# Second layer of the second mixture: seven half-size products in place of eight for 1792 of 2304 tokens

## The chip, the cores and the metric

The kernel runs on one core of a Trainium2 chip. Its time is the device time of one execution in microseconds, given as the median of several runs.

## What is computed

An attention (pooled and local) gives `x` of 2304 tokens by 512. Two feed-forward mixtures follow, both 512 to 2048 to 512. The change is in the last product of the second.

```python
def _moe2_ref(x, w_in, w_out, s, b) -> np.ndarray:
    h = x @ w_in
    r = np.maximum(h, 0.0)
    g = s * (r * r) + b
    return (g @ w_out).astype(np.float32)
```

All is float32. The kernel makes one float32 product from three matmuls in a reduced format: each operand is cut into a high part and the small rest, and high by high, high by low and low by high are summed.

## The kernel before

Five engines work beside each other: TensorE (PE; its weight loads are listed as PEld), VectorE (DVE), ScalarE (ACT), GpSimd (hardly used) and the queue of SyncE (SP), which issues nearly all transfers.

The kernel writes down its operations with `op(engine, cost, function, w, r, pr)`: what is written and read, and a priority. A planner (`Weave.plan`) then places them one by one on the engines by these costs, and this fixes the order in which each engine executes. Buffers come from named kinds with a fixed number of slots; for kinds in the list given to `Weave`, buffers take slots in the order in which they were written down. An engine executes in its order: an instruction that waits holds up all that stand behind it. An operation of `EITHER` may be placed on ACT or DVE.

Tokens go in blocks of 512 (the last of 256). The second mixture has two stages.

**Its first layer** (`group`, `late`, `w_sums`) already uses seven products in place of eight. It writes `g` to HBM (`g_dram`, listed as `gd`). `w_sums` loads a plain weight tile `f` of 128x512 into one of four staging slots (kind `st`), makes sums and cuts them into high and low parts.

**Its second layer** runs over blocks and, in each, over the 16 slices of 128 of the 2048 features. Per slice and block: `graw` comes back from HBM, ACT casts it to `gh`, DVE subtracts to `gl`, and PE makes, for each of 128 tokens, one product of three matmuls with 512 columns into one of four PSUM banks `o`. The stationary operand is a 128x128 tile of `gh` or `gl`; the 512 columns are a weight tile `wo`. All 16 `wo` tiles (high and low) are made once, in the first block, by `w_out` and `halves`, and stay in SBUF. Finished banks are copied to `os` and stored.

```python
def product(t, n, lhs, rhs, w, r, first, last, pr, **kw):

    def fn():
        for i in range(3):
            nc.tensor.matmul(t(), lhsT=lhs(i), rhs=rhs(i), start=(first and i == 0), stop=(last and i == 2), **kw)
```

That `product` is line 831 of the profile; all matmuls of both mixtures are recorded under it. Line 1112 is the cast to `gh`, line 1113 the subtraction to `gl`, line 387 the low half of a weight tile, line 996 a sum of `w_sums`, line 327 a copy or cast on either engine, line 340 a transfer.

Of the kernel before, what the change touches and what calls it, by code (L numbers as in the profile page):

```python
# [8 lines left out]
F32 = mybir.dt.float32  # L9
# [7 lines left out]
P = 128  # L17
CH = 18
# [253 lines left out]
def kernel(ctx, tc, q, k, v, w1_in, w1_out, w2_in, w2_out, s2, b2, cst, out):  # L272
# [37 lines left out]
    W = Weave(kinds, ("lq", "lk", "lv", "xf", "xh", "xl", "upT", "sc", "le", "bank", "u", "yr", "st"))  # L310
# [28 lines left out]
    def dma(out, in_, eng=None, **kw):  # L339
        (eng or nc.sync).dma_start(out=out, in_=in_, **kw)  # L340
# [44 lines left out]
    def halves(f, o, pr, more=0.0):  # L385
        op(EITHER, (0.52 + more, 0.34 + more), lambda eng: copy(eng, o[:, 0], f[:].bitcast(F32)), w=[(o, 0)], r=[f], pr=pr)
        op("dve", 0.6 + more, lambda: nc.vector.tensor_tensor(
            out=o[:, 1], in0=f[:].bitcast(F32), in1=o[:, 0].bitcast(F32), op=ALU.subtract), w=[(o, 1)], r=[f, (o, 0)], pr=pr - 0.001)
# [444 lines left out]
        op("pe", 3 * pe(n), fn, w=w, r=r, pr=pr, table="mix")  # L833
# [153 lines left out]
    def plain(nm, m, kind, after, pr):  # L987
        f = Buf(kind, [P, KD, P], F32, "f32")
        op("sp", (1, 0.8), lambda: dma(f[:], w_dram[nm][m]), w=[f], r=[(w_dram[nm], m)] + after, pr=pr)
        return f  # L990

    def w_sums(m, pr, after):
        f, g = [plain("in", m + a * HF, "st", after, pr) for a in range(2)]
        d, e = [Buf("st", [P, KD, P], F32, "sum") for _ in range(2)]
        def plus(out, a, b, by, w, r):
            op("dve", dve(2 * P) + MORE, lambda: nc.vector.tensor_tensor(out=out(), in0=a(), in1=b(), op=by), w=[w], r=r, pr=pr)

        half = lambda t, i: (lambda: t[:, 2 * i:2 * i + 2])
# [91 lines left out]
    wo2 = {}  # L1090

    def w_out(m, pr):
        f = plain("out", m, "st", [(sums[HF - 1][3], 0)], pr)
        wo2[m] = Buf("u", [P, 2, KD, P], F32R, "wo")
        halves(f, wo2[m], pr, MORE)

    for j, (c0, n) in enumerate(blocks):
        nt = n // P
        os_ = [Buf("bank", [P, DM], F32, f"o{d}") for d in range(nt)]
        for q in range(HF):  # L1100
            if j == 0:
                w_out(q, 40 + 2 * q)
                w_out(q + HF, 41 + 2 * q)
            graw = Buf("u", [P, 2, n], F32, "graw")
            op("sp", (1, 1.6 * n / NB), lambda graw=graw, q=q, j=j: dma(graw[:], g_dram[j].tile[q::HF].rearrange("f p n -> p f n")),
               w=[graw], r=[(g_dram[j], q), (g_dram[j], q + HF)], pr=41 + 20 * j + 2 * q)
            for a in range(2):
                m = q + a * HF
                wo = wo2[m]
                gh = Buf("gh", [P, n], F32R, "gh2")  # L1110
                gl = Buf("gl", [P, n], F32R, "gl2")
                op("act", act(n), lambda graw=graw, gh=gh, a=a: nc.scalar.copy(out=gh[:], in_=graw[:, a]), w=[gh], r=[graw], pr=-5 + j * 0.1)  # L1112
                op("dve", dve(n), lambda graw=graw, gh=gh, gl=gl, a=a: nc.vector.tensor_tensor(  # L1113
                    out=gl[:], in0=graw[:, a], in1=gh[:].bitcast(F32), op=ALU.subtract), w=[gl], r=[graw, gh], pr=-5 + j * 0.1)
                for d in range(nt):
                    sl = slice(d * P, (d + 1) * P)
                    product(lambda d=d, os_=os_: os_[d][:], DM, lambda i, gh=gh, gl=gl, sl=sl: (gl if i == 2 else gh)[:, sl],
                            lambda i, wo=wo: wo[:, i % 2].rearrange("p k f -> p (k f)"), [os_[d]], [wo, gh, gl], q == 0 and a == 0, q == HF - 1 and a == 1,
                            LP + 300 + j * 10)
        for d in range(nt):  # L1120
            o = Buf("ys", [P, DM], F32, "os")
            op(EITHER, (act(DM), dve(DM)), lambda eng, o=o, d=d, os_=os_: copy(eng, o[:], os_[d][:]),
               w=[o], r=[os_[d]], pr=-5)
            r0 = c0 + d * P
            whole = min(max(NBAND * S - r0, 0), P)

            def store(o=o, r0=r0, whole=whole):
                if whole:
                    dma(out[r0:r0 + whole], o[:whole])
                for i in range(whole // NCH, P // NCH):  # L1130
                    b, r = divmod(r0 + i * NCH, S)
                    dma(out[b * S:(b + 1) * S].rearrange("(c s) e -> s c e", s=CH)[r // NCH], o[i * NCH:(i + 1) * NCH])

            op("sp", (1 if whole == P else 4, 0.9), store, r=[o], pr=-5)
# [49 lines left out]
```

## Time and profile before

| | |
|---|---|
| median of 3 runs | 906.52 us (904.98 to 906.55) |
| the profiled execution | 908.74 us, its span 906.9 us |
| granted TensorE clock, mean | 0.995 |
| PE busy | 879.2 us (97%) |
| DVE busy | 664.3 us (73%) |
| ACT busy | 441.6 us (49%) |

The span runs from the first to the last instruction in the trace; the execution's own time has 1.84 us more around it. Busy times are sums over the span, so they tell nothing of single stages.

### The profile page before, as it was taken

How to read it: one execution, taken by the hardware profiler on the slowest of the kernel's cores; microseconds unless marked ns; L12 is line 12 of the kernel's file. 1: busy time of each engine (PE TensorE's matmuls, PEld its weight loads, DVE VectorE, ACT ScalarE, POOL GpSimd, SP SyncE). 2: the span in 40 equal slices, each digit the busy share in tenths (PEclk: the TensorE clock that was granted, in tenths of full speed). 3: DMA queues.
4: the chain of work that ended last, by engine and by line, in shares of the span. 5: the costliest groups of instructions: out<-in, count | busy, mean ns of one | idle time of the engine just before them, and what ended most of it. 6: DMA issues, size and time to landing. Idle time of an engine off the chain costs nothing.

```text
span 906.9 us, 13852 instructions
## 1 busy us (share of the span) xinstructions
PE 879.2 (97%) x5016; PEld 718.2 (79%) x5016; DVE 664.3 (73%) x1266; ACT 441.6 (49%) x956; POOL 0.2 (0%) x4
## 2 busy tenths in 40 slices
PE   7899999999999999999999999999999999999997
PEld 6677767777777877787878988888888888888885
DVE  6999997799999999898778988777687322222222
ACT  5965785755547323432234665555567322223232
POOL 0000000000000000000000000000000000000000
PEclk9989999999999999999999999999999999999999
DMA  9999312453333221446998433434279962201011
GB/s 192 257 296 252 108 44 56 134 150 89 113 81 83 93 73 33 139 153 217 301 311 282 136 105 128 154 140 136 105 243 329 385 227 93 70 24 30 17 36 35
DMA packets 129389, 132.66 MB, mean 146 GB/s; under 512 B 64684, under 2 KB 90922, under 8 KB 129322
## 3 DMA queue, kind: packets, MB, share of 16 engines
q1 hardware_dynamic: 129010, 131.49, 47.7%
q8 instruction: 39, 0.64, 0.3%
q10 hardware_dynamic: 312, 0.30, 0.1%
q14 instruction: 28, 0.23, 0.1%
HBM read 95.06 MB, written 36.70 MB: 145 GB/s over the span
## 4 chain that ended last, share of the span: by engine, by line
PE 58%; DVE 27%; DMA 7%; ACT 4%; issue 3%; SPq 1%; DVEq 0%; ACTq 0%
PE o L831 22%; PE ha L831 10%; PE hp L831 10%; PE y L831 7%; PE hc L831 5%; DVE tmp L513 3%; DMA w_raw<-in_moe_w_out_dram 2%; DVE gl L853 2%; PE hb L831 2%; DVE tmp L476 2%; DVE f L381 2%; DVE sc L479 2%; DVE f L378 2%; DVE tmp L518 2%; DVE f L375 1%
## 5 line engine op out<-in xcount | busy, mean ns | idle before, releaser
L831 PE MATMUL hp<-xh,wi 128*128 128x512 f32 (+1 forms) x640 | 201.6, 379 | 2.2 <-ACT g L851 1.6
L831 PE MATMUL y<-gh,wo 128*128 128x512 f32 (+1 forms) x640 | 201.1, 377 | 0.0
L831 PE MATMUL o<-wo,gh 128*128 128x512 f32 x576 | 177.3, 389 | 0.0
L1113 DVE TENSOR_TENSOR gl<-graw,gh 128x512 fp32r<-128x512 f32 (+1 forms) x80 | 51.0, 639 | 136.4 <-ACT gh L1112 130.3
L831 PEld LDWEIGHTS hp<-xh,wi 128*128 128x128 f32 x640 | 117.1, 189 | 27.2 <-ACT g L851 6.2
L831 PEld LDWEIGHTS y<-gh,wo 128*128 128x128 f32 x640 | 117.1, 189 | 19.4 <-issue 0.4
L831 PEld LDWEIGHTS o<-wo,gh 128*128 128x128 f32 x576 | 108.1, 188 | 22.4
L831 PE MATMUL y<-gl,wo 128*128 128x512 f32 (+1 forms) x320 | 118.9, 372 | 2.7 <-DVE gl L853 2.5
L831 PE MATMUL hp<-xl,wi 128*128 128x512 f32 (+1 forms) x320 | 118.6, 371 | 1.0 <-DVE xl L554 1.0
L1112 ACT CAST gh<-graw 128x512 fp32r<-128x512 f32 (+1 forms) x80 | 46.4, 581 | 135.6 <-PE o L831 135.3
L831 PE MATMUL o<-wo,gl 128*128 128x512 f32 x288 | 112.0, 389 | 0.0
L852 ACT CAST gh<-g 128x512 fp32r<-128x512 f32 (+1 forms) x80 | 46.2, 577 | 94.6 <-PE y L831 93.0
L831 PE MATMUL ha<-yh,wi 128*128 128x512 f32 x256 | 87.1, 390 | 0.0
L851 ACT ACTIVATE g<-hp 128x512 f32<-128x512 f32 (+1 forms) x80 | 44.5, 556 | 61.6 <-DVE gl L853 56.7
L831 PEld LDWEIGHTS y<-gl,wo 128*128 128x128 f32 x320 | 60.5, 189 | 13.9 <-DVE gl L853 5.8
L831 PEld LDWEIGHTS hp<-xl,wi 128*128 128x128 f32 x320 | 60.5, 189 | 9.6 <-DVE xl L554 1.6
L831 PEld LDWEIGHTS o<-wo,gl 128*128 128x128 f32 x288 | 54.1, 188 | 11.3
L1013 DVE SCALAR_TENSOR_TENSOR g<-g 128x512 f32<-128x512 f32 (+1 forms) x80 | 49.4, 635 | 10.5 <-ACT g L1012 9.6
L831 PEld LDWEIGHTS ha<-yh,wi 128*128 128x128 f32 x256 | 48.1, 188 | 9.6
L853 DVE TENSOR_TENSOR gl<-g,gh 128x512 fp32r<-128x512 f32 (+1 forms) x80 | 50.4, 630 | 4.1 <-ACT gh L852 3.9
L831 PE MATMUL ha<-yl,wi 128*128 128x512 f32 x128 | 50.0, 390 | 0.0
L327 ACT COPY g<-ha 128x512 f32<-128x512 f32 x47 | 27.6, 587 | 42.1 <-PE ha L831 37.7
(153 smaller groups left out, 1351.0 us busy)
## 6 DMA issues: line engine op xcount, KB each, us to landing
gd<-g SPq DMA_DIRECT2D x64, 256.0 KB
graw<-gd SPq DMA_DIRECT2D x32, 512.0 KB
wi_raw<-in_moe_w_in_dram SPq DMA_DIRECT2D x16, 512.0 KB
wo_raw<-in_moe_w_out_dram SPq DMA_DIRECT2D x16, 512.0 KB
w_raw<-in_moe_w_in_dram SPq DMA_DIRECT2D x16, 512.0 KB
w_raw<-in_moe_w_out_dram SPq DMA_DIRECT2D x16, 512.0 KB
nq<-in_q_dram SPq DMA_DIRECT2D x32, 144.0 KB
nk<-in_k_dram SPq DMA_DIRECT2D x32, 144.0 KB
```

Source lines behind the costliest of these rows:

```text
L327: (nc.scalar.copy if eng == "act" else nc.vector.tensor_copy)(out=out, in_=in_)
L378: op("dve", 0.6 + more, lambda: nc.vector.scalar_tensor_tensor(out=f[:], in0=t[:, :, :, 1], scalar=-0x40000000, in1=f[:], op0=ALU.bitwise_ ...
L381: op("dve", 0.6 + more, lambda: nc.vector.scalar_tensor_tensor(out=f[:], in0=t[:, :, :, 0], scalar=29, in1=f[:], op0=ALU.logical_shift_rig ...
L476: op("dve", dve(n * WIN * D), lambda t=t, i0=i0, n=n, h2=h2: nc.vector.tensor_tensor(out=t[:], in0=wide(qs[:, h2, i0:i0 + n, :].unsqueeze( ...
L513: op("dve", dve(n * WIN * D), lambda t=t, i0=i0, n=n, h2=h2: nc.vector.tensor_tensor(out=t[:], in0=wide(e[:, h2 * ns + i0:h2 * ns + i0 + n ...
L831: nc.tensor.matmul(t(), lhsT=lhs(i), rhs=rhs(i), start=(first and i == 0), stop=(last and i == 2), **kw)
L851: op("act", act(n), lambda g=g, hp=hp: nc.scalar.activation(out=g[:], in_=hp[:], func=AF.Silu), w=[g], r=[hp], pr=-5, table="silu")
L852: op("act", act(n), lambda g=g, gh=gh: nc.scalar.copy(out=gh[:], in_=g[:]), w=[gh], r=[g], pr=-5)
L853: op("dve", dve(n), lambda g=g, gh=gh, gl=gl: nc.vector.tensor_tensor(out=gl[:], in0=g[:], in1=gh[:].bitcast(F32), op=ALU.subtract), w=[gl ...
L1013: op("dve", dve(n) + 1.5 * MORE, lambda: nc.vector.scalar_tensor_tensor(out=t[:], in0=t[:], scalar=0.0, in1=t[:], op0=ALU.max, op1=ALU.mul ...
L1112: op("act", act(n), lambda graw=graw, gh=gh, a=a: nc.scalar.copy(out=gh[:], in_=graw[:, a]), w=[gh], r=[graw], pr=-5 + j * 0.1)
L1113: op("dve", dve(n), lambda graw=graw, gh=gh, gl=gl, a=a: nc.vector.tensor_tensor(out=gl[:], in0=graw[:, a], in1=gh[:].bitcast(F32), op=ALU ...
```

## The change

The first block of 512 tokens is left as it was (eight tiles by the full 512 columns). The other 1792 tokens go in seven groups of 256. In a group, `g` is a 2 by 2 matrix of quarters (two halves of 128 tokens, two halves of 1024 features), and so is `w_out` (two halves of the features, two halves of 256 columns). Seven products of quarters (`prod`, each 8 feature slices of three matmuls with 256 columns, 24 matmuls) give the result, in place of eight. `mix` makes the sums of quarters of `g` on DVE (eight operations of 128x512 for each group); `parted` cuts each of 14 half-quarters into high and low; `snap` and `join` bring the banks `oa`, `ob`, `oc` (256 columns each) together in SBUF. The sums of the weights (`t12`, `t43`) are made in `out_sums` while the first layer of the second mixture still runs, written to HBM (`w2t`), and are later loaded and cut like the plain tiles (`split_out`).

```diff
+    kinds["u2"] = kinds["u"] + kinds["lk"] + kinds["lv"] + kinds["tmp"]
+    kinds["hk"] = sum((kinds[t] for t in ("gh", "gl", "g", "lq", "upT")), [])
+    kinds["ok"] = kinds["ys"] + kinds["st"]
...
+    def out_sums(q, pr, after):
+        f, g = [plain("out", q + a * HF, "st", after, pr) for a in range(2)]
+        d = Buf("st", [P, KD, P], F32, "sum")
...
+            op("dve", dve(2 * P) + MORE, lambda: nc.vector.tensor_tensor(out=out(), in0=a(), in1=b(), op=ALU.subtract), w=[w], r=r, pr=pr)
+
+        minus(lambda: half(d, 0), lambda: half(f, 1), lambda: half(f, 0), (d, 0), [f])
+        minus(lambda: half(d, 1), lambda: half(g, 1), lambda: half(d, 0), (d, 1), [(g, 1), (d, 0)])
+        minus(lambda: half(g, 1), lambda: half(g, 1), lambda: half(f, 1), (g, 1), [f])
+        minus(lambda: half(g, 0), lambda: half(g, 0), lambda: half(d, 1), (g, 0), [(d, 1)])
+        for nm, t in (("t12", d), ("t43", g)):
+            op("sp", (1, 0.8), lambda nm=nm, t=t: dma(w_dram[nm][q], t[:]), w=[(w_dram[nm], q)], r=[t], pr=pr)
...
     for m in range(1, HF):
         w_sums(m, 20 + m, last)
+        out_sums(m - 1, 24 + m, last)
+    out_sums(HF - 1, 24 + HF, last)
...
+        def prod(bank, g, name, new):
+            for q in range(HF):
+                hi, lo = g[q // QT]
+                w, wb = wcomb[name, q]
+                product(lambda: bank[:], 2 * P, lambda i, q=q, hi=hi, lo=lo: (lo if i == 2 else hi)[:, q % QT, :], lambda i, w=w: w(i % 2),
+                        [bank], [hi, lo, wb], new and q == 0, q == HF - 1, LPP, skip_group_check=True)
...
+        prod(ba, parted(a11, 0), "b11", True)
+        snap(o1, 0, ba)
+        mix(ss, a21, a22, ALU.add, 0.01)
+        prod(bc, parted(ss, 0.01), "t1", True)
+        mix(ss, ss, a11, ALU.subtract, 0.02)
+        prod(ba, parted(ss, 0.02), "t2", False)
+        snap(o1, 1, ba)
+        prod(bb, parted(a12, 0.03), "b21", True)
+        join(o1, 0, bb)
+        mix(a21, a11, a21, ALU.subtract, 0.04)
+        prod(ba, parted(a21, 0.04), "t3", False)
+        snap(o2, 0, ba)
+        join(o2, 1, bc, 0)
+        prod(bb, parted(a22, 0.05), "t4", True)
+        join(o2, 0, bb)
+        mix(ss, a12, ss, ALU.subtract, 0.06)
+        prod(bc, parted(ss, 0.06), "b22", False)
+        join(o1, 1, bc)
```

On PE, near the end of the first block, before (`o` with four numbers are the four token tiles of a block):

```order
L831 MATMUL o_7845<-wo,gl_8021 128x512
L831 MATMUL o_7853<-wo,gh_8016 128x512 x2
L831 MATMUL o_7853<-wo,gl_8021 128x512
L831 MATMUL o_7833<-wo,gh_8034 128x512 x2
L831 MATMUL o_7833<-wo,gl_8039 128x512
```

and of the change, at the place where the first group begins to come between the slices of the first block:

```order
L834 MATMUL o_7645<-wo,gh_7880 128x512 x2
L834 MATMUL o_7645<-wo,gl_7885 128x512
L834 MATMUL oa<-wo,gh 128x256 x2
L834 MATMUL oa<-wo,gl 128x256
...
L834 MATMUL o_7592<-wo,gh_7899 128x512 x2
L834 MATMUL o_7592<-wo,gl_7918 128x512
```

The last five slices of the first block have 9 or 12 matmuls of the first group between them; after it, the groups follow in runs of 24 matmuls with 256 columns on one bank.

On DVE, in the middle of the second layer, before (one subtraction after another, now and then a copy):

```order
L1113 TENSOR_TENSOR gl_8131<-graw,gh_8125 128x512
L327 COPY os<-o_7853 128x512
L1113 TENSOR_TENSOR gl_8154<-graw,gh_8149 128x512
```

and of the change, within one group (line 1158 is `parted`, 1151 `mix`, 1179 `join`, 330 `snap`):

```order
L330 COPY os<-oa 128x256
L1158 TENSOR_TENSOR gl<-graw,gh 128x512 x2
L1179 TENSOR_TENSOR os<-ob,os 128x256
L1151 TENSOR_TENSOR gs<-graw 128x512
L1158 TENSOR_TENSOR gl<-graw,gh 128x512
L1151 TENSOR_TENSOR gs<-graw 128x512
L1158 TENSOR_TENSOR gl<-gs,gh 128x512
L1151 TENSOR_TENSOR graw<-graw 128x4x128
L1158 TENSOR_TENSOR gl<-gs,gh 128x512
L1179 TENSOR_TENSOR os<-oc,os 128x256
```

`mix` and `join` now stand between the subtractions, mostly one by one.

On SP, where the first layer's last `g` is stored, before:

```order
L340 DMA gd_94<-g_7480 128x512
L340 DMA graw<-gd_92 128x2x512 x3
L340 DMA graw<-gd_93 128x2x512 x8
L340 DMA graw<-gd_94 128x2x512 x8
```

and of the change (`gd_93` is the first block's `g`, `gd_94` the next one's):

```order
L343 DMA gd_96<-g_7573 128x512
L343 DMA f_7682<-w2t_91 128x512
L343 DMA f_7689<-w2t_92 128x512
L343 DMA graw<-gd_93 128x2x512
L343 DMA graw<-gd_94 128x4x256
L343 DMA f_7708<-w2out 128x512
L343 DMA f_7717<-w2out 128x512
L343 DMA graw<-gd_94 128x4x256 x3
L343 DMA f_7762<-w2t_91 128x512
L343 DMA graw<-gd_93 128x2x512
```

Nine weight tiles are still to be loaded there, where before only `graw` was left; the order of all engines ahead of the second mixture's first layer is the same in both.

## Rows read from the trace of the kernel before

**Rows 1.** Busy time by stage: engine busy us (instructions), granted clock, DMA share, GB/s.
```profile
520.00:702.00 182.00, 182.00 (x931) 155.99 (x930) 137.98 (x246) 109.98 (x194) 0.00 (x0) 1.00 0.49 167
702.00:746.00 44.00, 44.00 (x196) 36.44 (x195) 13.13 (x19) 12.36 (x20) 0.00 (x0) 1.00 0.86 310
746.00:901.00 155.00, 155.00 (x684) 128.02 (x683) 42.74 (x68) 43.92 (x77) 0.00 (x0) 1.00 0.15 44
...
480.00:520.00 40.00, 38.22 (x311) 37.45 (x311) 34.25 (x64) 23.64 (x52) 0.00 (x0) 1.00 0.59 199
...
715.00:720.00 5.00, 5.00 (x24) 4.14 (x23) 1.39 (x2) 1.25 (x2) 0.00 (x0) 1.00 1.05 390
```

**Rows 2.** The chain that ended last, in order of time: its last pieces.
```profile
706.55 194.49 PE o L831 x858
901.04 0.02 issue
901.07 0.59 ACT os L327
```

**Rows 3.** Instructions of the second layer by shape: count, busy us, mean ns, idle before.
```profile
L831 PE MATMUL o<-wo,gh 128*128 128x512 f32 x576 | 177.3, 389 | 0.0
L831 PE MATMUL o<-wo,gl 128*128 128x512 f32 x288 | 112.0, 389 | 0.0
...
L1113 DVE TENSOR_TENSOR gl<-graw,gh 128x512 fp32r<-128x512 f32 x62 | 42.9, 692 | 120.2 <-ACT gh L1112 114.1 <-PE o L831 6.1
L1112 ACT CAST gh<-graw 128x512 fp32r<-128x512 f32 x62 | 38.7, 624 | 120.1 <-PE o L831 120.1
```

**Rows 4.** PE in order of time: matmuls with 512 columns.
```profile
880.24 0.39 PE L831 MATMUL o<-wo,gl 128*128 128x512 f32 x1
880.47 0.61 PE L831 MATMUL o<-wo,gh 128*128 128x512 f32 x2
...
888.40 0.39 PE L831 MATMUL o<-wo,gl 128*128 128x512 f32 x1
```

**Rows 5.** PE, then its weight loads, in order of time: 256 columns (block 4).
```profile
487.73 0.28 PE L831 MATMUL hp<-xh,wi 128*128 128x256 f32 x1
487.85 0.28 PE L831 MATMUL y<-gh,wo 128*128 128x256 f32 x1
...
491.69 0.40 PE L831 MATMUL y<-gh,wo 128*128 128x256 f32 x2
...
487.74 0.19 PEld L831 LDWEIGHTS y<-gh,wo 128*128 128x128 f32 x1
487.86 0.19 PEld L831 LDWEIGHTS y<-gl,wo 128*128 128x128 f32 x1
```

**Rows 6.** Start and end of the last matmul, last copies and stores.
```profile
900.39 1.26 ACT L327 COPY os<-o 128x512 f32<-128x512 f32 x2 [1.86 <-PE o L831]
...
900.64 0.39 PE L831 MATMUL o<-wo,gl 128*128 128x512 f32 x1
901.00 3.61 SPq L340 DMA_DIRECT2D out_dram<-os  x8
```

**Rows 7.** Instructions of the first layer's stage by shape, 520 to 702 us.
```profile
L387 DVE TENSOR_TENSOR wo<-f,wo 128x512 fp32r<-128x512 f32 x16 | 10.8, 689 | 1.7 <-ACT wo L327 1.6
...
L327 ACT CAST wo<-f 128x512 fp32r<-128x512 f32 x13 | 7.9, 618 | 2.7 <-DMA f<-w2out 2.0 <-PE ha L831 0.7
...
L996 DVE TENSOR_TENSOR sum<-sum,f 128x256 f32<-128x256 f32 x7 | 2.9, 421 | 0.1
...
L950 DVE TENSOR_TENSOR yt<-yt 128x512 f32<-128x512 f32 x4 | 2.7, 685 | 0.0
...
L327 ACT COPY ys<-y 128x256 f32<-128x256 f32 x3 | 1.0, 373 | 0.1
```

**Rows 8.** DVE reads in broken patterns: durations min/median/max, and a mean.
```profile
L476 DVE TENSOR_TENSOR tmp<-lq,lk x28: 1080/1544/1559, 183.2 to 387.5; 128x1344 f32<-128x1344 f32 x16, 128x896 f32<-128x896 f32 x12
...
L538 DVE TENSOR_TENSOR xf<-pt,upT 128x128 f32<-128x128 f32 x36 | 12.1, 386 | 0.0
```

**Rows 9.** The first weight-tile load of the second layer, and the first cast.
```profile
658.77 0.92 SPq L340 DMA_DIRECT2D f<-w2out  x2
...
663.05 0.42 DVE L327 CAST wo<-f 128x512 fp32r<-128x512 f32 x1
```

More of the change, by code (lines that the diff above doesn't have):

```diff
@@ L309 @@
     kinds["ct"] = sum((kinds[t] for t in ("lq", "lk", "lv", "tmp", "upT", "g", "gh", "gl", "ys")), [])
[L310 removed]
+    kinds["hk"] = sum((kinds[t] for t in ("gh", "gl", "g", "lq", "upT")), [])
+    kinds["ok"] = kinds["ys"] + kinds["st"]
+    W = Weave(kinds, ("lq", "lk", "lv", "xf", "xh", "xl", "upT", "sc", "le", "bank", "u", "u2", "yr", "st", "hk", "ok"))
     op = W.op
@@ L976 @@
     sums = {}
-    w_dram = {nm: fixed(drp, [KF, P, KD, P], F32, f"w2{nm}") for nm in ("in", "out")}
+    w_dram = {nm: fixed(drp, [n, P, KD, P], F32, f"w2{nm}") for nm, n in (("in", KF), ("out", KF), ("t12", HF), ("t43", HF))}
     def whole(nm, m, pr):
@@ L1008, in w_sums, with minus @@
         sums[m] = got
+    def out_sums(q, pr, after):
+        f, g = [plain("out", q + a * HF, "st", after, pr) for a in range(2)]
+        d = Buf("st", [P, KD, P], F32, "sum")
+        half = lambda t, i: t[:, 2 * i:2 * i + 2]
+        def minus(out, a, b, w, r):
+            op("dve", dve(2 * P) + MORE, lambda: nc.vector.tensor_tensor(out=out(), in0=a(), in1=b(), op=ALU.subtract), w=[w], r=r, pr=pr)
[5 more added lines that the diff above has]
+            op("sp", (1, 0.8), lambda nm=nm, t=t: dma(w_dram[nm][q], t[:]), w=[(w_dram[nm], q)], r=[t], pr=pr)
     def late(f, t, u, n, first):
@@ L1088 @@
         group(m, s, 300 + i)
[L1090 to L1134, printed above, removed]
@@ new lines, with parts, split_out @@
+    QT = HF // 2
+    wo2, wcomb = {}, {}
+    st_gate = [(sums[HF - 1][3], 0)]
+    def parts(f, o, pr, c, keys, n):
+        op(EITHER, (act(n) + MORE, 0.07 + n / 1920.0 + MORE), lambda eng: copy(eng, o(0), f()), w=keys, r=c, pr=pr)
+        op("dve", dve(n) + MORE, lambda: nc.vector.tensor_tensor(out=o(1), in0=f(), in1=o(0).bitcast(F32), op=ALU.subtract), w=keys, r=c + keys, pr=pr - 0.001)
+    def split_out(nm, m, pr):
+        f = plain(nm, m, "st", st_gate, pr)
+        o = Buf("u2", [P, 2, KD, P], F32R, "wo")
+        parts(lambda: f[:], lambda x: o[:, x], pr, [f], [o], DM)
+        return o
@@ new lines, with named, g_load @@
+    flat = lambda t, x, j: t[:, x, 2 * j:2 * j + 2].rearrange("p k f -> p (k f)")
+    def named(q, *parts):
+        for nm, o, j in parts:
+            wcomb[nm, q] = (lambda x, o=o, j=j: flat(o, x, j), o)
+    graw = {}
+    def g_load(p, pr):
+        u, at = divmod(p * 2 * P, NB)
+        for i in range(2):
+            for h in range(2):
+                t = Buf("u2", [P, QT, 2 * P], F32, "graw")
+                f0 = i * HF + h * QT
+                op("sp", (1, 1.6), lambda t=t, f0=f0, u=u, at=at: dma(t[:], g_dram[u].tile[f0:f0 + QT, :, at:at + 2 * P].rearrange("f p n -> p f n")),
+                   w=[t], r=[(g_dram[u], f) for f in range(f0, f0 + QT)], pr=pr)
+                graw[p, i, h] = t
@@ new lines, in put, with store @@
+    def put(o, r0):
+        whole = min(max(NBAND * S - r0, 0), P)
+        def store():
+            if whole:
+                dma(out[r0:r0 + whole], o[:whole])
+            for i in range(whole // NCH, P // NCH):
+                b, r = divmod(r0 + i * NCH, S)
+                dma(out[b * S:(b + 1) * S].rearrange("(c s) e -> s c e", s=CH)[r // NCH], o[i * NCH:(i + 1) * NCH])
+        op("sp", (1 if whole == P else 4, 0.9), store, r=[o], pr=-5)
+    n = blocks[0][1]
+    NG = NT // (2 * P)
@@ new lines @@
+    q = HF
+    named(q - 1, ("b11", wo2[q - 1], 0), ("b21", wo2[q - 1 + HF], 0), ("b22", wo2[q - 1 + HF], 1))
+    o = split_out("t12", q - 1, 41.2 + q)
+    named(q - 1, ("t1", o, 0), ("t2", o, 1))
+    o = split_out("t43", q - 1, 41.3 + q)
+    named(q - 1, ("t4", o, 0), ("t3", o, 1))
+    for d in range(n // P):
+        o = Buf("ok", [P, DM], F32, "os")
+        op(EITHER, (act(DM), dve(DM)), lambda eng, o=o, d=d: copy(eng, o[:], os_[d][:]), w=[o], r=[os_[d]], pr=-6)
+        put(o, d * P)
@@ L1135 @@
+    for p in range(g0, NG):
+        if p + 1 < NG:
+            g_load(p + 1, 61 + p)
+        out_group(p, -5 + 0.1 * p)
     W.run()
```

57 lines of the change are left out of this document (added).

## The prediction

> **What bounds the kernel now.** I read the stages first, then the chain that ended last, then the groups of instructions by shape, then PE in order of time. The busy times by stage [rows 1] show PE busy for 182.00 of 182.00 us in the second mixture's first layer, 44.00 of 44.00 in the first block of its second layer and 155.00 of 155.00 in the rest, all at a granted clock of 1.00. The reader is to see that nothing makes PE wait there, while DVE has 42.74 of 155 us of work in the last stretch. The chain that ended last [rows 2] agrees: 194.49 us of matmuls into `o` in one piece, then a copy of 0.59 us and the stores. DVE's and ACT's idle time in that stage [rows 3] is a wait for PE: the cast waits 120.1 us for a buffer that PE gives back, and the subtraction for the cast. So this stage is worth as many microseconds as its matmuls take, and fewer matmul columns are fewer microseconds as long as PE stays fed.
>
> **Matmuls removed and added.** The second layer has 576 + 288 = 864 matmuls with 512 columns [rows 3]. Four of 18 token tiles stay, so 192 remain and 672 go. Their pace: in one stretch the matmul at 880.24 and the one at 888.40 stand 36 matmuls apart [rows 4], (888.40 - 880.24) / 36 = 0.2267 us each. Removed: 672 x 0.2267 = 152.3 us. (The 0.39 us of one matmul overlaps with its neighbours; the pace counts.)
>
> Added: 7 groups of 7 products of 24 matmuls = 1176 matmuls with 256 columns. Block 4 of the first mixture runs such matmuls already: from 487.73 to 491.69 there are 33 of them without a wait, in the same 128*128 by 256 shape, 3.96 / 33 = 0.1200 us each [rows 5]. Added: 1176 x 0.1200 = 141.1 us. That is 11.2 us less. Seven eighths of the columns would give 19.0 us; the 0.013 us that a matmul costs beyond half of the larger one's pace takes the rest, since there are 504 more matmuls. Each has a weight load of 0.19 us, and in the same stretch loads start every 0.12 us, one with each matmul [rows 5]: they are hidden at this width.
>
> Here a rule speaks against the change. The Trainium skill, page "TensorE: Matmul & The Clock Gate", says in Part 3 (The mechanism) that a weight load overlaps with a running matmul only when the two use different row groups, and in Part 2 (LDWEIGHTS) that a load takes its columns divided by 1.2 per ns, an estimated 107 ns for 128 columns. All matmuls here use all rows, so by that page the 504 additional loads would cost an estimated 54 us and the change would lose some 43 us. The trace disagrees: at that rule a matmul with 256 columns could not follow the last after 0.1200 us.
>
> **The end.** The last matmul starts at 900.64 and the span ends at 906.9, 6.26 us later. In between are two copies, and eight store instructions that SP issues in 3.61 us from 901.00, 0.45 each, which leaves 906.9 - 904.61 = 2.29 us for the last to land [rows 6]. After the change one `join` of 256 columns and four stores follow the last matmul (the other half tile is complete one product earlier). A matmul with 256 columns ends 0.28 after its start [rows 5], the copy followed its matmul's end by 0.04 [rows 2], a DVE operation of 256 takes 0.42 [rows 7], SP followed the copy within 0.02: 0.28 + 0.04 + 0.42 + 0.02 + 4 x 0.45 + 2.29 = 4.85. That saves 1.4 us.
>
> **Work put beside PE, at nothing.** (a) `out_sums`: 32 DVE subtractions of 256 at 0.421 us [rows 7] are 13.5 us in the first layer's stage, where DVE works 137.98 of 182 us [rows 1]; it rises to 83%. It also issues 16 loads and 16 stores of 256 KB, 8.4 MB in 182 us, 46 GB/s on top of 167, where 390 GB/s has been moved [rows 1]. What hides it is DVE's 44 us of idle time there; if that cover were gone, all 13.5 us could appear on PE. Bounds 0 and 13.5; I take 0, because DVE's gaps are three times the work and the PSUM banks leave PE several products ahead. The work cannot gain time there.
>
> (b) `split_out`: 16 further tiles, each a cast of 0.618 on ACT and a subtraction of 0.689 on DVE [rows 7], 11.0 us on DVE; they fall mostly between 660 and 745, where PE has 43.5 us of the first block (192 x 0.2267) as cover. Their loads share four staging slots. A load was followed by its cast after 663.05 - 658.77 = 4.3 us [rows 9], so with the split of 1.3 us a slot turns in about 5.6 us and four slots give a tile every 1.4 us. On SP nine of these loads, and five loads of `graw`, stand behind the last store of `g`, so the ninth tile is cut some 15 to 20 us after that store, around 728, and the first Strassen product of sums is wanted after 745. Taken: 0.
>
> (c) The groups. Each has 168 x 0.1200 = 20.16 us of PE. DVE has 14 subtractions at 0.692 [rows 3], 8 sums at 0.685 [rows 7], and four joins and about one copy at 0.42: 9.7 + 5.5 + 2.1 = 17.3 us, 86%. ACT has 14 casts at 0.624 and two copies at 0.373 [rows 3, 7], 9.5 us. So PE remains the longest. The eight slots of kind `hk` hold four half-products, each 1.44 us of PE. When one half ends, cast and subtraction of the half four places on need 0.62 + 0.69 plus small gaps, and PE wants it 4.31 us after that moment: about 2.9 us are left over for what stands in front on DVE, and the order puts a sum or a join between the subtractions mostly one by one. Not shown in the trace is a sum that reads quarters in runs of 128 elements, and a join from PSUM of 256. Near bound: reads in runs of 64 elements take 1544 ns for 1344 elements [rows 8], no more for each than the 685 ns for 512 whole ones. Far bound: the add from PSUM in a scattered pattern takes 386 ns for 128 elements [rows 8], where the line through 421 for 256 and 689 for 512 gives 287, so 1.34 times. I take the near one, as the runs are like its runs.
>
> **The sum.** 152.3 - 141.1 + 1.4 = 12.6 us. The profiled execution took 908.74, so 896.1 on its scale; it lies 2.2 us above the median of the runs shown, so the median should be 906.52 - 12.6 = 893.9 us.
>
> **Rivals.**
>
> *PE waits at the halves without a sum (gives back some of the gain).* Six of a group's 14 halves have no sum in front, and DVE may idle there. If all their spare time were lost, the other eight would have 17.3 - 6 x 0.69 = 13.2 us of DVE for 11.5 us of PE, 1.7 us for each group, 12 us over seven: 905.5, no change. Against it: the slots reach four halves ahead, so spare time is mostly usable. Half of the loss gives 899.7.
>
> *The switch from the first block.* Loads on SP wait for staging slots, and behind a waiting load stand the `graw` of the next group. For it: the nine loads; against it: some 17 us of margin as worked out in (b). If the margin fails by a few microseconds: 897 to 899.
>
> *`out_sums` appears on PE.* A subtraction that waits for its load holds up the joins behind it on DVE, and SP's stores of `g` stand behind a store of sums. A part of the 13.5 us: 897 to 907.4.
>
> *DVE becomes the bound of the groups (slower).* Place: the seven groups. If the reads of quarters cost the far bound of (c), 22 operations take 15.2 x 1.34 = 20.4 and DVE needs 22.5 us for each group against 20.16 of PE: 2.3 x 7 = 16 us lost, 910. It decides from 20.16 + 14.4 / 7 = 22.2 us on, beyond which the change is slower than before by over 0.2%. Against it: the near bound of [rows 8].
>
> *The weight loads are not hidden at this width (slower, far).* 504 more loads at up to 0.19 us [rows 5] would be 95 us, so up to 989. The pace of block 4 excludes nearly all of it; the page named above stands for this rival.
>
> **How the numbers follow.** Forecast near 894: 0.62. Waits at the halves: 0.14 in part, 0.03 in full (no change). The switch: 0.05. `out_sums`: 0.07, of which 0.05 faster, 0.01 same, 0.01 slower. DVE as the bound: 0.07. Weight loads: 0.02. A difference under 0.2%, 1.8 us, is about what a measurement of this kernel cannot tell from no change. Faster 0.62 + 0.14 + 0.05 + 0.05 = 0.86, same 0.04, slower 0.10. The forecast's own range is 892 to 897 (a pace of 0.1185 to 0.1215 is 1.8 us either way, and the end may be worth less). For 8 in 10 it reaches to the partial waits: 891.5 to 901.5.
>
> **What the profile will show.** If I am right: 1176 matmuls with 256 columns at 0.120 us apart, PE busy throughout from 520 to about 890, the first layer's stage ending at the same time, DVE near 86% in the groups with its waits still for ACT and PE, and about 4.9 us from the last matmul to the end. Wrong would be: PE idle time released by DVE `gl` in the groups, sums on DVE clearly above 0.69 us, PE waiting for `wi` before 702, a pace above 0.125, or waits for the load of `graw` or of a weight tile around 745.

## The result: 896.66 us, and the profile after

The changed kernel takes 896.66 us (median of 4 runs, 895.67 to 899.32) against 906.53 for the kernel before on the same chip, a ratio of 0.9893 with a 95% interval of 0.9861 to 0.9925. That is faster, inside the range (891.5 to 901.5) and 2.8 us above the predicted 893.9. Its profiled execution took 895.92, with a span of 894.1.

The stages of the changed kernel, columns as in [rows 1]:

```profile
520.00:702.00 182.00, 180.95 (x914) 153.84 (x913) 145.84 (x273) 111.73 (x197) 0.00 (x0) 1.00 0.63 208
702.00:746.00 44.00, 44.00 (x206) 36.68 (x206) 26.70 (x42) 20.87 (x36) 0.00 (x0) 1.00 0.75 251
746.00:890.00 144.00, 143.77 (x1177) 142.58 (x1175) 109.82 (x185) 63.44 (x110) 0.00 (x0) 1.00 0.33 101
```

PE is busy to the end in the second layer (the 0.23 us missing in the last row lie behind the last matmul). DVE has gone from 42.74 of 155 us to 109.82 of 144 and still has room. The row to stop at is the first: PE stood for 1.05 us in the first layer's stage, where before it did not stand at all.

The chain that ended last, start and length, with its last pieces:

```profile
688.96 4.56 DMA f<-w2t
694.91 4.46 DMA f<-w2t
706.28 31.42 PE o L834 x138
...
800.49 2.88 PE oa L834 x24
803.37 2.88 PE ob L834 x24
...
886.89 2.89 PE oc L834 x24
```

Each product of quarters is 24 matmuls in 2.88 us, 0.1200 each, as in [rows 5]. Ahead of them the chain passes through two loads of weight sums (`w2t`), which the kernel before did not have.

To add up the difference, four marks are enough: the first matmul into `hp` (the work begins), the first into `ha` (the first layer of the second mixture), the last into `hc` (its end), and the last matmul of all. One tile's matmuls in the kernel before (count, min/median/max ns, first and last start):

```profile
L831 PE MATMUL hp<-xh,wi x640: 278/389/628, 33.5 to 524.9; 128*128 128x512 f32 x128, 128*128 128x256 f32 x32
L831 PE MATMUL ha<-yh,wi x256: 389/389/396, 522.2 to 704.8; 128*128 128x512 f32 x128
L831 PE MATMUL hc<-yh,wi x128: 389/389/389, 533.5 to 706.2; 128*128 128x512 f32 x128
```

and in the changed kernel:

```profile
L834 PE MATMUL hp<-xh,wi x640: 277/389/796, 31.5 to 522.8; 128*128 128x512 f32 x128, 128*128 128x256 f32 x32
L834 PE MATMUL ha<-yh,wi x256: 388/389/499, 520.0 to 704.5; 128*128 128x512 f32 x128
L834 PE MATMUL hc<-yh,wi x128: 388/389/498, 531.3 to 705.9; 128*128 128x512 f32 x128
```

The last matmuls start at 900.64 [rows 6] and at 889.49 (below). So, in us:

| from, to | before | after | difference | predicted |
|---|---|---|---|---|
| start of the span, first `ha` | 522.2 | 520.0 | -2.2 | 0 |
| first `ha`, last `hc` (layer stage) | 184.0 | 185.9 | +1.9 | 0 |
| last `hc`, last matmul (second layer) | 194.4 | 183.6 | -10.8 | -11.2 |
| last matmul, end of the span (tail) | 6.3 | 4.6 | -1.7 | -1.4 |
| span | 906.9 | 894.1 | -12.8 | -12.6 |

The first line is not the change's: the order of all engines is the same there, and the first matmul into `hp`, at 33.5 and 31.5, already shows the 2 us. In the thirteen profiles of this study that mark lies between 31.5 and 35.5, and in the nine with this order the first `ha` lies between 520.0 and 525.3: the profile of before (522.2) stands in the middle, and that of the changed kernel is the earliest. What the change does by itself is the sum of the other three lines, 10.6 us less. (Six matmuls into `o` stand ahead of the last `hc` in both; in *sums_only* and *from_256* they are nine, 0.68 us more.)

The tail, in order of time:

```profile
887.38 4.60 SPq L343 DMA_DIRECT2D out_dram<-os  x8
...
889.49 0.28 PE L834 MATMUL oc<-wo,gl 128*128 128x256 f32 x1
889.81 0.42 DVE L1179 TENSOR_TENSOR os<-oc,os 128x256 f32<-128x256 f32 x1 [2.45 <-PE oc L834]
```

The first store was issued 2.11 us before the last matmul began, since the other half tile was complete; the eight issues end at 891.98, and 2.1 us later the span ends.

### The profile page after: what moved, and what is told of

Same layout as the page of the kernel before. It is cut to its first block, busy times and chain, and to the rows that moved or that the text cites. A ratio compares the mean times of both kernels' runs of the same rounds, so it can differ in the third digit from the quotient of the medians.

```text
span 894.1 us, 15244 instructions
## 1 busy us (share of the span) xinstructions
PE 868.0 (97%) x5520; PEld 731.6 (82%) x5520; DVE 754.8 (84%) x1436; ACT 471.7 (53%) x1009; POOL 0.2 (0%) x4
## 4 chain that ended last, share of the span: by engine, by line
PE 51%; DVE 29%; DMA 9%; ACT 4%; issue 3%; SPq 2%; DVEq 0%; ACTq 0%
PE ha L834 9%; PE hp L834 8%; PE oa L834 7%; PE o L834 5%; PE y L834 5%; PE ob L834 5%; PE oc L834 5%; PE hc L834 4%; DVE tmp L516 4%; DMA w_raw<-in_moe_w_out_dram 3%; DVE gl L856 3%; DVE tmp L479 3%; SPq L343 2%; DVE f L381 2%; PE hb L834 2%
## 5 line engine op out<-in xcount | busy, mean ns | idle before, releaser
L834 PEld LDWEIGHTS y<-gh,wo 128*128 128x128 f32 x640 | 117.2, 189 | 19.4 <-issue 0.4
L834 PE MATMUL oa<-wo,gh 128*128 128x256 f32 x336 | 61.4, 283 | 0.0
L1157 ACT CAST gh<-graw 128x512 fp32r<-128x512 f32 x56 | 34.7, 620 | 42.4 <-PE ob L834 19.7
L1158 DVE TENSOR_TENSOR gl<-graw,gh 128x512 fp32r<-128x512 f32 x56 | 38.6, 690 | 19.9 <-ACT gh L1157 18.7
L834 PEld LDWEIGHTS oa<-wo,gh 128*128 128x128 f32 x336 | 52.6, 192 | 0.2
L834 PE MATMUL oa<-wo,gl 128*128 128x256 f32 x168 | 47.6, 283 | 0.0
L1036 ACT ACTIVATE g<-g,sbt 128x512 f32<-128x512 f32 (+1 forms) x60 | 45.2, 772 | 3.7 <-DVE g L1031 3.4
```

The costliest lines, as they stand in the source:

```text
L1036: nc.scalar.activation(out=t[:], in_=t[:], func=AF.Identity, scale=sbt[:, 0:1], bias=sbt[:, 1:2])
L1157: op("act", act(4 * P) + MORE, lambda x=x, hi=hi: nc.scalar.copy(out=hi[:], in_=x()), w=[hi], r=[xk], pr=pr + n)
L1158: op("dve", dve(4 * P) + MORE, lambda x=x, hi=hi, lo=lo: nc.vector.tensor_tensor(out=lo[:], in0=x(), in1=hi[:].bitcast(F32), op=ALU.subtra ...
```

## The experiments

All were timed beside the kernel before on the same chip, in three groups: *again* to *eight_narrow*, *planned_longer* to *four_slots*, *layer_longer* to *from_256*. Layer stage, second layer and tail are cut at the marks above, from one profile each; where the planner made another order at the start of the layer stage, the first cut means something else and is left out.

| kernel | median, us (runs) | before | ratio to before [95%] | layer stage | second layer | tail |
|---|---|---|---|---|---|---|
| again | 898.0 (6) | 906.76 | 0.9911 [0.9892, 0.9929] | 186.3 | 184.0 | 4.7 |
| sums_only | 909.04 (12) | 906.76 | 1.0016 [1.0, 1.0031] | 186.5 | 193.8 | 6.4 |
| sums_later | 897.88 (6) | 906.76 | 0.9888 [0.9865, 0.9911] | 186.2 | 183.5 | 4.6 |
| eight_narrow | 917.39 (4) | 906.76 | 1.0123 [1.0103, 1.0144] | 184.0 | 203.6 | 6.1 |
| planned_longer | 898.88 (6) | 908.09 | 0.991 [0.9887, 0.9933] | | 188.3 | 4.6 |
| sums_twice | 901.24 (4) | 908.09 | 0.9934 [0.9909, 0.9959] | 184.8 | 188.8 | 4.7 |
| half_twice | 896.56 (4) | 908.09 | 0.9882 [0.9858, 0.9906] | 184.9 | 184.5 | 4.6 |
| four_slots | 909.13 (10) | 908.09 | 1.0015 [0.9998, 1.0032] | 186.0 | 195.8 | 4.6 |
| layer_longer | 896.16 (4) | 906.75 | 0.9887 [0.9869, 0.9905] | | 183.5 | 4.6 |
| layer_longer_later | 893.41 (4) | 906.75 | 0.986 [0.9838, 0.9882] | | 183.4 | 4.6 |
| from_256 | 902.35 (10) | 906.75 | 0.995 [0.9935, 0.9966] | | 190.5 | 4.8 |

### again: the change unaltered, with more rounds

No edit.

> The changed kernel, unaltered, for a narrower interval. By the stages of the two profiles the change gains 11.0 us after the first layer, 1.5 us at the end and loses 1.9 us in the first layer: 10.6 us, a ratio of 0.9883. If the 12.6 us of the forecast hold and the first four runs were high by chance, 0.986.

898.0 us, 8.8 less than before. Its profile has the same pieces: layer stage +2.3, second layer -10.4, tail -1.6, in all 9.7 less. Its second layer is 0.4 longer than that of the first profile because PE comes late to three matmuls of the first block between 723 and 727, the first of them behind `gl`.

### eight_narrow: the price of the narrower matmuls alone

The kernel before, with each product with 512 columns of blocks 1 on made as two with 256:

```diff
-                    product(lambda d=d, os_=os_: os_[d][:], DM, ...
+                    for c in range(1 if j == 0 else 2):
+                        cw = DM if j == 0 else DM // 2
+                        cs = slice(c * cw, (c + 1) * cw)
+                        product(lambda d=d, os_=os_, cs=cs: os_[d][:, cs], cw, ...
```

> The kernel before with each product of the blocks after the first made as two of 256 columns: eight products at the width of the change, 1344 matmuls of 256 columns for 672 of 512. By the pace of block 4 they take 1344 x 0.1200 = 161.3 us for 152.3: 9.0 us slower, so that seven for eight alone is worth 20 us. If weight loads were not hidden at this width, 672 more of them at 0.1 to 0.19 us would add 70 to 128 us.

This kernel serves for its time alone: what it leaves in the banks is not the right product (relative error 0.146), while the matmuls, their columns and their weight loads are those meant. The second layer takes 203.6 us against 194.4, 9.2 more for 672 matmuls that became 1344. PE in order of time:

```profile
849.77 0.28 PE L831 MATMUL o<-wo,gl 128*128 128x256 f32 x1
849.89 0.40 PE L831 MATMUL o<-wo,gh 128*128 128x256 f32 x2
...
851.93 0.28 PE L831 MATMUL o<-wo,gl 128*128 128x256 f32 x1
```

From 849.77 to 851.93 there are 18 matmuls, 0.1200 us each: this work too pays the 0.0133 us for each doubling that the prediction took from block 4, 672 x 0.0133 = 9.0. So of the 19.0 us that an eighth of the columns is worth, the narrower shape takes 7.8, and the rest is the change's.

On the additional weight loads the prediction set two things against each other. The Trainium skill, page "TensorE: Matmul & The Clock Gate", Part 3 (The mechanism), lets a load overlap a running matmul only if the row groups differ; 672 more loads at its estimated 107 ns would be 72 us, and 9.2 were measured. Part 2 of the same page (Step-by-step: what each phase is for) also allows a load to be pulled ahead when it goes to the weight buffer in the background, and so does Part 3 itself a few lines before; the prediction left this second case out. The measurement agrees with it and not with the first.

### sums_only: the weight sums alone, their results unused

The kernel before with `out_sums` of the change added:

```diff
+    def out_sums(q, pr, after):
...
         w_sums(m, 20 + m, last)
+        out_sums(m - 1, 24 + m, last)
+    out_sums(HF - 1, 24 + HF, last)
```

> The kernel before with the 32 subtractions, 16 loads and 16 stores of out_sums added and their result left unused; the second layer stays at eight products. If the 1.9 us lost in the first layer's stage come from out_sums, the time rises by 1 to 2 us and PE shows waits for ACT's copies of ha before 660 us. If they come from the loads of the sums (f from w2t) with their casts, which this kernel does not have, the time stays within 0.5 us and PE has no wait in that stage. Cover gone altogether would be up to 13.5 us.

909.04 us, 1.0016 of before: the sums cost 1.5 us by the ratio, with an interval that begins at nothing, and 2.5 by the layer stage of the profile (186.5 against 184.0), of which 0.68 are three more matmuls into `o` ahead of the mark. The rows show how. On SP, ACT, DVE and PE (engine, line, operation; in brackets the idle time before it and what ended it):

```profile
618.61 0.38 SPq L340 DMA_DIRECT2D f<-w2in  x1
...
619.57 0.38 SPq L340 DMA_DIRECT2D w2t<-sum  x1
620.40 0.32 SPq L340 DMA_DIRECT2D f<-w2in  x1
...
623.79 0.62 ACT L327 CAST wi<-f 128x512 fp32r<-128x512 f32 x1 [1.85 <-DMA f<-w2in]
624.32 1.07 ACT L327 COPY g<-ha 128x512 f32<-128x512 f32 x2
...
619.95 0.42 DVE L1016 TENSOR_TENSOR f<-f,f 128x256 f32<-128x256 f32 x1
...
624.30 0.39 PE L831 MATMUL ha<-yh,wi 128*128 128x512 f32 x1
624.95 0.50 PE L831 MATMUL ha<-yh,wi 128*128 128x512 f32 x1 [0.26 <-ACT g L327]
```

Read it from the end. PE's matmul at 624.95 waits for ACT to empty its bank, the copy at 624.32. That copy stands behind a cast of a weight tile, which waited 1.85 us for its load, and the load was issued at 620.40. It takes a staging slot, and `out_sums` holds three of the four (`f`, `g` and the sum); at 620.37 the subtraction `f<-f,f` ends (619.95 + 0.42), and the load goes out at once. That the slot was this one is read from the 0.03 us between the two; no run had more staging slots, so this step is not shown by an experiment. None of the three engines was short of time: ACT executes in order, and a load that is late for a cast is late for the copy behind it.

The bracket is not the whole cost. Where PE doesn't wait, matmuls of this shape start 0.2267 us apart. From 624.30 to 624.95 it is 0.65, and the next one follows at 0.34 (625.29), so the place cost 0.53. Two more, at 679.70 and 692.26, cost 0.81 and 0.38 by the same reckoning.

### The same in the changed kernel, and three edits against it

PE and ACT of the changed kernel, in order of time:

```profile
623.04 0.39 PE L834 MATMUL ha<-yh,wi 128*128 128x512 f32 x1
623.71 0.50 PE L834 MATMUL ha<-yh,wi 128*128 128x512 f32 x1 [0.29 <-ACT g L330]
...
699.40 0.39 PE L834 MATMUL hc<-yh,wi 128*128 128x512 f32 x1
700.55 0.50 PE L834 MATMUL ha<-yh,wi 128*128 128x512 f32 x1 [0.76 <-ACT g L330]
...
699.39 0.62 ACT L330 CAST wo<-f 128x512 fp32r<-128x512 f32 x1 [0.84 <-DMA f<-w2t]
699.91 0.58 ACT L330 COPY g<-ha 128x512 f32<-128x512 f32 x1
```

The first place is that of *sums_only*. The second has the same form with another load: the cast at 699.39 belongs to `split_out`, and its `w2t` load is the one in the chain above, 694.91 + 4.46 = 699.37. By the reckoning above the two places lose 0.55 and 1.03 us, most of the 1.9.

*sums_later* loads and cuts the weight sums only after all plain tiles:

```diff
-            o = split_out("t12", q - 1, 41.2 + q)
-            named(q - 1, ("t1", o, 0), ("t2", o, 1))
-            o = split_out("t43", q - 1, 41.3 + q)
-            named(q - 1, ("t4", o, 0), ("t3", o, 1))
...
+    for nm, names in (("t12", ("t1", "t2")), ("t43", ("t4", "t3"))):
+        for q in range(HF):
+            o = split_out(nm, q, 50 + q)
+            named(q, (names[0], o, 0), (names[1], o, 1))
```

> The change with the 16 tiles of weight sums loaded and cut only after all plain tiles and the loads of the first block's g, instead of between them. If ACT's casts that wait for these loads hold up its copies of ha near 699 us, the waits of PE between 680 and 710 (0.76 us in the records, about 1 us with the restart) go and the time falls by 1 us against the change; the first Strassen product may wait for a sum around 750 if 17 us of margin were too few. If the waits come from out_sums, nothing changes.

897.88 us, no gain over *again* beyond the intervals. The wait did not go, it moved: PE waited 0.66 us at 693.48, behind a cast that waited 2.41 us, until 692.32, for its load of a plain tile (`w2out`). The first place, at 626.27, was longer than in the change (0.67 us). The likely reason, not tested by itself, is that loads queue for the same four slots whichever of them is first.

*planned_longer* tells the planner that a tile's load takes twice as long, for all tiles from the second mixture on, so that the casts are placed later on ACT:

```diff
-        op("sp", (1, 0.8), lambda: dma(f[:], w_dram[nm][m]), ...
+        op("sp", (1, 0.8 if pr < 20 else 1.6), lambda: dma(f[:], w_dram[nm][m]), ...
```

> The change with one number of the planner altered: a weight load (line of plain) from w_sums of slice 1 on is planned with 1.6 us of moving time in place of 0.8. Nothing is added or removed; the planner places the casts that wait for these loads later on ACT, and the copies of ha no longer stand behind a waiting cast. If that is how out_sums costs PE its 1.9 to 2.3 us, the waits of PE for ACT between 520 and 710 go (0 to 0.3 us left), the stage from the first ha to the last hc falls from 185.9 back to about 184 us, and the time falls by 1.5 to 2 us against the change. If the loss is due to DVE having too much to do there, it stays.

It cures the one stage and harms the next. PE is busy for 186.00 of 186.00 us between 520 and 706, but the second layer takes 188.3 us, 4.7 more than after. PE's waits there, with total, times and longest:

```profile
PE o L834 <- ACT gh L1229: 2.8, 2, 1.4
```

At the first of the two places ACT's cast to `gh` waited 4.72 us for a `graw` load, at the second it stood behind the cast of a weight sum that waited 3.06 us for its load: loads of both kinds now come too late.

*layer_longer* says the same for the first layer's tiles and those of `out_sums` alone, and *layer_longer_later* adds the edit of *sums_later* to it:

```diff
-        op("sp", (1, 0.8), lambda: dma(f[:], w_dram[nm][m]), ...
+        op("sp", (1, 1.6 if 20 < pr < 40 else 0.8), lambda: dma(f[:], w_dram[nm][m]), ...
```

> As planned_longer, but the longer moving time (1.6 us) only for the loads of w_sums and out_sums; the loads of the second layer's tiles are planned as in the change, so that the switch to the second layer should stay as it was. If late loads ahead of the copies of ha are the cause, PE's waits for ACT between 600 and 660 go, those near 700 (behind a cast that waits for a second-layer tile) may stay: 0.3 to 1.2 us, and the time falls by 1 to 2 us against the change, to a ratio near 0.987 against before. The second layer keeps its 183.6 to 184.0 us.

> The two edits of layer_longer and sums_later together. If the two kinds of wait add, PE has none left between 520 and 710 and this is 0.5 to 1 us faster than layer_longer; if the wait near 700 comes from plain tiles as well (as in sums_later), no difference.

With *layer_longer* the place near 624 is gone and the one at 700 stays (0.84 us at 700.26): 896.16 us. With both, no wait is left in the layer stage:

```profile
520.00:708.00 188.00, 187.95 (x942) 160.07 (x942) 150.17 (x279) 108.67 (x191) 0.00 (x0) 1.00 0.62 210
708.00:752.00 44.00, 44.00 (x222) 37.54 (x221) 30.45 (x50) 22.90 (x40) 0.00 (x0) 1.00 0.75 251
```

893.41 us, the best of all kernels here: 0.986 of before, and below *again* (0.9911) with intervals that do not meet, though it overlaps with that of the first measurement of the change (0.9893) and with that of *layer_longer* (0.9887).

The layer stage of these kernels can be compared after all: between the same two marks they have 894 matmuls in place of 930, because 36 with 256 columns now stand ahead of the first `ha`. Without any loss that is 184.0 - 36 x 0.1200 = 179.7 us. *planned_longer* takes 179.7 (525.3 to 705.0), *layer_longer* 181.2 (524.4 to 705.6) and *layer_longer_later* 180.0 (522.9 to 703.0). So the longer planning can give the whole loss back with all the added work still in place, which shows that the loss comes from the order and not from the amount of work. The 1.2 us between the last two agree with the wait at 700.26 (0.84 in the bracket, about 0.27 for the restart).

That each of the two places has a cause and an edit of its own is not shown. PE's wait for ACT near 624 (0.26 to 0.67 us) is in five of the seven profiles with `out_sums` and the old planning and in none of the four with the longer one. But the wait near 700 is also missing in *half_twice*, whose first layer is ordered as in the change, and in *planned_longer* and *from_256*, which lack the edit of *sums_later*.

### sums_twice and half_twice: how much room DVE has in the groups

After each half of a sum of quarters (in *half_twice*: after the first half only) DVE makes one more operation of the same size that leaves the values as they are:

```diff
+                op("dve", dve(4 * P) + MORE, lambda o=o: nc.vector.tensor_tensor(out=o(), in0=o(), in1=o(), op=ALU.max), w=[ok], pr=pr + n)
```

> The change with a second DVE instruction of 128x512 after each of the eight sums of a group (the maximum of the sum with itself, same output). DVE then has 17.3 + 8 x 0.69 = 22.8 us for a group in which PE has 20.16. If DVE's load alone decides, as the rival of the slower side said (from 20.16 on), the groups take 22.8 us each and the time rises by 2.6 x 7 = 18 us, a little less for the last group. If the queue order made DVE late earlier than its load does, more than 18.

> The same with a second instruction after only one of the two half sums: 17.3 + 4 x 0.69 = 20.05 us of DVE for a group, 99% of PE's 20.16. If buffers reach far enough that only the load counts, the time is that of the change within 2 us; if DVE's waits for the cast and for banks cannot be used for sums (the rival of the halves without a sum, up to 1.7 us per group), 5 to 15 us slower than the change.

Eight additional operations for each group cost 5.0 us in the second layer (188.8 against the mean of 183.8 of the change's two profiles), far from the 18 that the load in durations had given; four cost 0.7, about the spread. One stretch of 20 us inside the groups in *sums_twice*:

```profile
800.00:820.00 20.00, 19.46 (x162) 19.25 (x162) 18.69 (x33) 8.95 (x17) 0.00 (x0) 1.00 0.43 134
```

in *half_twice*:

```profile
800.00:820.00 20.00, 20.00 (x169) 20.00 (x169) 17.79 (x31) 9.35 (x17) 0.00 (x0) 1.00 0.43 132
```

and in the changed kernel:

```profile
800.00:820.00 20.00, 20.00 (x169) 20.00 (x168) 15.90 (x28) 9.22 (x16) 0.00 (x0) 1.00 0.41 127
```

The change itself, at 15.9, is not near the place where PE begins to wait. DVE in order of time shows why it is 15.9 and not 17.2, the 86% of the prediction:

```profile
780.71 0.68 DVE L1151 TENSOR_TENSOR gs<-graw 128x512 f32<-128x512 f32 x1
781.31 0.69 DVE L1158 TENSOR_TENSOR gl<-graw,gh 128x512 fp32r<-128x512 f32 x1
781.91 0.69 DVE L1151 TENSOR_TENSOR gs<-graw 128x512 f32<-128x512 f32 x1
782.51 0.69 DVE L1158 TENSOR_TENSOR gl<-gs,gh 128x512 fp32r<-128x512 f32 x1
```

Each lasts 0.68 to 0.69 us, but they start 0.60 apart: when nothing separates them, the next begins before the last has ended. Six windows of 20 us from 760 to 880 have 16.0 of 20 on average, so a group of 20.16 us has 16.1 of DVE.

In *sums_twice* PE waits at one place in each of five groups, 20.9 to 21.0 us apart, and DVE stands twice in a group for a join whose bank PE has not finished:

```profile
803.98 0.42 DVE L1180 TENSOR_TENSOR os<-ob,os 128x256 f32<-128x256 f32 x1 [0.46 <-PE ob L834]
...
809.74 0.42 DVE L1180 TENSOR_TENSOR os<-ob,os 128x256 f32<-128x256 f32 x1 [0.80 <-PE ob L834]
...
819.12 0.39 PE L834 MATMUL oa<-wo,gl 128*128 128x256 f32 x1 [0.54 <-DVE gl L1159]
```

Each place costs 0.80 us with the restart, 4.0 in all; another 1 us lies in the first block, where PE waits 0.69 us for `gl` at 712.87. By distances the load alone would still fit: 30 operations at 0.60 and four joins at 0.34 are 19.4 us, under PE's 20.16. What goes beyond is the 1.3 us in which DVE stands for the two joins. So it is the order on DVE, on top of the load, that makes PE wait here.

### four_slots: the lead of the halves

The kind `hk`, from which the high and low halves come, is cut to four slots (two half-products in place of four):

```diff
-    kinds["hk"] = sum((kinds[t] for t in ("gh", "gl", "g", "lq", "upT")), [])
+    kinds["hk"] = sum((kinds[t] for t in ("gh", "gl")), [])
```

> The change with four slots in place of eight for high and low parts in the groups (only gh and gl), two halves of a product in place of four. When a half ends, its slots take the half two places on: cast 0.62, subtraction 0.69 and gaps are 1.4 us, and PE wants it after 1.44 us, with 0.5 us of sums and joins in front on DVE for each half. If the lead of four halves is what hides DVE and ACT, PE waits 0.1 to 0.7 us at each of 98 halves: 10 to 70 us slower. If two halves are enough, the time stays.

909.13 us, the whole gain gone (1.0015 of before). PE's waits in the second layer:

```profile
PE o L834 <- DVE gl L1230: 5.2, 10, 1.4
PE ob L834 <- DVE gl L1158: 2.3, 5, 0.5
```

Most of it is in the first block, whose own `gh` and `gl` take slots that are now all that the groups have (in its last slices ACT's cast to `gh` waits 2.8 us for PE each time); in the groups PE is busy 19.5 to 19.95 of 20 us. There the first group no longer comes between the slices either: the first matmul into `oa` starts at 762.0, after the last into `o` at 761.8. From there to the last matmul at 907.1 it is 145.1 us, 4 more than seven times 20.16. So the groups live with a lead of two, at some cost, and the lead is worth most in the first block.

### from_256: eight groups

*layer_longer* with only 256 tokens left to the eight products:

```diff
-    n = blocks[0][1]
+    n = 2 * P
...
-... dma(raw[:], g_dram[0].tile[q::HF].rearrange("f p n -> p f n")),
+... dma(raw[:], g_dram[0].tile[q::HF, :, :n].rearrange("f p n -> p f n")),
```

> layer_longer with seven products from token 256 on: eight groups, and only two tiles by the full columns. PE's work falls by 96 x 0.2267 - 168 x 0.1200 = 1.6 us. If the tiles and sums of the weights arrive in time with half the cover (21.8 us in place of 43.5), 1.6 us faster than layer_longer; if loads, casts and staging slots cannot keep up (1.4 us a tile by the estimate of the prediction, 32 tiles from about 660 on), PE waits 2 to 10 us between 715 and 745 and it is slower.

One more group should save another 11.2 / 7 = 1.6 us, and it costs 6.2 against *layer_longer*: 902.35. Busy time by stretch:

```profile
720.00:724.00 4.00, 4.00 (x19) 3.26 (x18) 1.79 (x4) 1.89 (x4) 0.00 (x0) 1.00 0.90 302
724.00:726.00 2.00, 1.89 (x14) 1.60 (x13) 1.90 (x3) 1.31 (x3) 0.00 (x0) 1.00 1.09 360
726.00:728.00 2.00, 0.55 (x5) 0.35 (x3) 1.03 (x3) 0.62 (x1) 0.00 (x0) 1.00 1.09 348
...
730.00:732.00 2.00, 0.84 (x4) 0.55 (x3) 0.60 (x1) 1.05 (x3) 0.00 (x0) 0.50 1.05 379
732.00:734.00 2.00, 1.98 (x5) 1.61 (x6) 1.92 (x5) 1.84 (x4) 0.00 (x0) 0.50 1.09 349
```

The first block is the cover under which most of the plain tiles and of the weight sums are loaded and cut. Halved, it ends before they are there. From 724 on the DMA engines are full (share 1.05 to 1.09), and PE waits for `gh` 1.45 us at 727.75 and 1.18 at 732.02. ACT is late with these casts for two reasons: it waits 1.65 us for a `graw` load ahead of the one at 727.08, and 3.06 us for a `w2t` load ahead of the cast that stands in front of the one at 731.57. After PE had been busy for 0.55 of 2 us, its granted clock fell from 1.00 to 0.50, the lower of the two levels (1.2 GHz), and stayed there for some 7 us: in that time matmuls with 512 columns start 0.43 apart. So the 512 tokens of the change are not caution but the cover of its own preparation.

## Why the prediction held, and where it did not

**Matmuls removed and added: right.** 11.2 us predicted, 10.8 and 10.4 in the two profiles of the change, and 11.0 in that of *layer_longer_later*. The paces of 0.2267 and 0.1200 carried over, and the weight loads are hidden; *eight_narrow* measured the surcharge by itself, 9.2 us for 9.0. One aside of the prediction does not come out: 504 more matmuls at 0.013 us are 6.6 us, not the 7.8 between 19.0 and 11.2. Those are 0.0067 us on each of the 1176 narrow matmuls; the sum itself does not use the aside.

**The end: right.** 1.4 predicted; 1.6 and 1.7 measured.

**(a) `out_sums` at nothing: wrong, by 0.6 to 1.8 us.** The step argued from DVE's gaps and from PSUM banks that keep PE ahead. DVE had the gaps. The cover failed elsewhere: four staging slots, a load that goes out when a slot comes free, ACT's order, and PE's bank behind it. The third rival, that `out_sums` appears on PE, had the right place but named DVE's joins and SP's stores as the way; it went by ACT's copies. Of its price (up to 13.5 us) little came true: 1.7 us at three places of *sums_only*, and 0.55 at one place of the change. The size differs between executions of one order: the whole layer stage grew by 1.9 and 2.3 in the change's two profiles and by 0.8, 0.9 and 2.0 in *sums_twice*, *half_twice* and *four_slots*, whose first layer is ordered alike.

**(b) `split_out` at nothing: right at the place that it looked at, wrong at another.** The margin before the groups held: PE is busy 44.00 of 44.00 from 702 to 746, and no load is waited for around 745. But the same tiles begin to be cut before 702, and there the cast at 699.39 held PE up for about 1 us. The second layer lost a little too: it takes 183.6 and 184.0 us in the change's two profiles and 183.4 in *layer_longer_later*.

**(c) The groups: right, with a size that was off.** The groups keep PE busy for 20.00 of 20 us. The 17.3 us of DVE were a sum of durations; measured are 16.1. The sums of quarters last 0.684 to 0.690 us, the near bound that was taken. So the rival of DVE as the bound was further off than its number said (*sums_twice* goes past it), and that of waits at the halves without a sum is refuted for eight slots. For four it shows: PE waits for `gl` in `ob`, whose two products have no sum in front, and stands 0.46 us at each of five such places, some 0.7 with the restart, against the 1.7 of the price.

**The sum and its scale.** 12.6 us predicted. The change gave 10.6 and 9.7 in the stages of its two profiles, 9.9 and 8.8 by the medians. Of the missing 2 to 4 us, the loss of the layer stage is 1.9 to 2.3 and the second layer 0.4 to 0.8; the rest is within the intervals. The difference of the two spans, 12.8 us, agrees with the forecast by luck: the profile of the changed kernel reached its first `ha` 2.2 us earlier, at the early end of the spread. The prediction did well to take its 12.6 us off the median and not off the profiled run of before. From the first `ha` on that run stands at the pace of its matmuls, so its 2.2 us above the median must lie ahead of it; what made them, no row settles.

Of the 2.8 us between the medians of *layer_longer* and *layer_longer_later* the profiles give 1.2 to the layer stage; 1.5 lie ahead of the first `ha` (524.4 and 522.9), in the spread that all kernels have there. Open: why the wait of *sums_later* at 693 is nearly as long as the one at 700 that it was to remove, why the places come and go between executions of one order, and whether more staging slots would remove them.

## What to carry to other kernels

When a product by seven takes the place of eight, price it in columns at the pace that the narrower matmul has in the trace: of 19 us the shape alone took 8. Work put into an engine's gaps is free only if its loads don't take the slots, and its casts the places, of work that a fuller engine waits for: follow each added load to the slot, the cast and the instruction behind that cast. For an engine that is near its limit take the distance from start to start and not the durations, and add the time that its own order makes it stand; and see where two executions part before a difference of their times enters a sum.

## What the runs showed of the hardware

DVE operations on 128x512 float32 values in SBUF last 0.69 us and start 0.60 us apart. The Trainium skill, page "VectorE: DVE Perf Modes" (The TRN2 errata), has both: a table value of 58 cycles plus the elements at 0.96 GHz, which is an estimated 594 ns, and a measured duration of 691 ns for such an operation; it calls the table too low as a duration, by a copy that took 693 ns. The rows here agree with both, the one as the distance and the other as the length.

After a wait the first matmul is listed with 0.50 us in place of 0.39, and the next follows 0.33 to 0.34 later in place of 0.2267: a wait of PE costs about 0.27 us more than its bracket shows (0.16 of it is the end of the matmul before, which otherwise lies under the next). A short one (0.29 in the bracket at 623.71) is then half unseen in a list of waits.
